# Second-layer products over 512 columns, first-layer row blocks in column groups of their own: an attention and soft-routing kernel on one core

## The chip, the cores and the metric

The kernel runs on one core of a Trainium2 chip. The metric is device time in microseconds (us) from start to end of one execution. The kernel before was timed three times: 200.5, 200.85 and 201.43 us, median 200.85. One execution was also recorded instruction by instruction; all durations below come from that record.

## The reference

Two stages follow each other. The first is an attention with a learned memory: for each of 8 x 8 heads, 576 positions are pooled into 32 memory slots, and the queries attend to those slots. The second is a soft mixture of eight experts over the 4608 rows that come out; the change is in its expert part:

```python
logits = x @ phi                       # x: 4608 x 512, phi: 512 x 32 slots
d = softmax(logits, axis=0)            # over the rows
slot_input = (d.T @ x).reshape(8, 4, 512)
for e in range(8):                     # 4 slots for each expert
    h = np.maximum(slot_input[e] @ w1[e], 0.0)     # 4 x 512 by 512 x 1024
    slot_out[e] = h @ w2[e]                        # 4 x 1024 by 1024 x 512
c = softmax(logits, axis=1)            # over the 32 slots
out = c @ slot_out                     # 4608 x 512
```

w1 and w2 are 16.8 MB each, all fp32. The inputs of the attention are about 33 MB, the output 9.4 MB.

## The kernel before

All data arrives and leaves through one queue, that of SyncE (SP). Its order is fixed when the program is built: attention inputs first, with weight pieces among them, then the rest of w1 and w2, then the stores. Weight pieces lie in a large arena in SBUF; a piece of w2 takes the place of a piece of w1 that TensorE (PE) has finished with, so a load of w2 waits for PE.

First layer (`expert_in`, L1376 to L1394). Each w1 matrix comes as two tiles of 1 MB. A tile holds two blocks of 128 input rows (c = 0, 1), and the 1024 hidden units are dealt into four sets (j). For a tile PE does 8 products of 256 columns. Each has 32 stationary columns (the expert's four slots, the rest zero), and `tile_position` puts the four sets into the four groups of 32 columns of the array. The two row blocks add up in PSUM. Four experts share a bank (EG = 4), so the layer runs in two halves of 64 products.

`hidden` (L1396 to L1421) then turns a half: ScalarE (ACT) copies it out of PSUM with relu, PE does two 128 x 128 transposes, VectorE (DVE) copies the result to hT.

Second layer (`mult`, `expert_out`, `tail_mult`). Each w2 matrix comes in two halves h of 4 row blocks. A product of one half and one half d of the 512 output columns is 4 matmuls of 256 columns in the four column groups, into `pacc[d]` (d = 0 in `kvbank`, d = 1 in `scbank`). Eleven halves are loaded whole. For the last five (NT = 5, the tails) `tail_out` loads the left 256 columns first, ten pieces of 256 KB, and then the right, ten more, so that the left half of the output can leave while the right is still on its way.

`slot_sums(d)` (L1345) copies `pacc[d]` to SBUF (`accs`), sums its four row groups by a product with `rep` (L1357), and splits the result into two fp32r parts in `sr` (L1364, L1369). `direct` (L1587) gives the first output rows straight from `accs`, `half_group` (L1603) the rest of two row groups column half by column half; DVE and ACT evict (L1579, L1580), SP stores (L1616).

The order on each engine is not that of the code: a planner (`Plan.order`) simulates costs given with each `add` and issues in the order that results. PE, ACT and DVE each do their list in order.

Of the kernel before, what the change touches and what calls it, by code (L numbers as in the profile page):

```python
# [253 lines left out]
def act(n, psum=True):  # L254
    return (0.16 if psum else 0.19) + n / 1200.0
# [15 lines left out]
def kernel(  # L271
# [1070 lines left out]
    sr = keep("sr", [P, 2, DM], dtype=F32R, parts=2)  # L1342
    so = [b_l.tile(), Tile(ap=kvbank[:, 1])]

    def slot_sums(d, middle=lambda: None):  # L1345
        x = slice(d * HD, d * HD + HD)
        add(
            *((ACT, act(HD)) if d else (DVE, dve(HD))),
            lambda: (nc.scalar.copy if d else nc.vector.tensor_copy)(
                accs.ap[:, x], pacc[d].ap[:, 0, :HD]  # L1350
            ),
            r=[pacc[d]], w=[accs.part(d)],
        )
# [13 lines left out]
        add(  # L1367
            DVE, dve(HD),
            lambda: nc.vector.tensor_tensor(  # L1369
                sr.ap[:, 1, x], so[d].ap[:, :HD], sr.ap[:, 0, x].bitcast(F32), op=ALU.subtract  # L1370
            ),
            r=[so[d], sr.part(d)], w=[sr.part(d)],
        )
        return z

    def expert_in(e, hb):  # L1376
        w1v = w1[e].rearrange("(i p z) f -> i p (z f)", i=2, z=2)
        w1b = [load_w(w1v[i], wqs if e == EG else ws) for i in range(2)]
        for i in range(2):

            def f(i=i):
                wv = w1b[i].ap.rearrange("p (c f) -> p c f", c=2)
                for c in range(2):
                    for j in range(4):
                        nc.tensor.matmul(  # L1385
                            hb.ap[NS * j: NS * j + NS, :256],
                            SIM.ap[:, 2 * i + c, NS * e: NS * e + NS],
                            wv[:, c].rearrange("p (x j t) -> p x j t", j=4, t=2)[:, :, j, :],
                            start=(e % EG == 0 and i == 0 and c == 0),
                            stop=(e % EG == EG - 1 and i == 1 and c == 1),  # L1390
                            tile_position=(0, NS * j),
                        )

            add(PE, (0.9, 32), f, r=[SIM, w1b[i]], w=[hb])  # L1394

    def hidden(g, hb):  # L1396
        hs, tp = hss.tile(), b_m.tile()

        add(
            ACT, act(256),  # L1400
            lambda: nc.scalar.activation(
                hs.ap.rearrange("p (t x) -> p t x", t=2),
                hb.ap[:, :256].rearrange("p (x t) -> p t x", t=2), AF.Relu,
            ),
            r=[hb], w=[hs],
        )
# [5 lines left out]
        add(PE, 2 * TP, f, r=[hs, ident_b], w=[tp])  # L1412
        x = slice(EG * g, EG * g + EG)
        add(
            DVE, dve(8 * EG * SE),
            lambda: nc.vector.tensor_copy(
                hT().rearrange("p x (e n) -> p x e n", e=E)[:, :, x, :SE],
                tp.ap[:, :256].rearrange("p (x e s) -> p x e s", x=8, e=E)[:, :, x],
            ),
            r=[tp], w=[hTb.part(g)],  # L1420
        )  # L1421

    tails = []

    def mult(dst, e, h, t, d):
        n = 2 if e < ONES else 4
        wide = t.ap.rearrange("p (j t d) -> p j t d", j=n, t=2)
        for k in range(2):
            for j in range(2):
                x, y = 2 * k + j, 2 * h + j  # L1430
                nc.tensor.matmul(
                    dst[NS * x: NS * x + NS, :HD],
                    hT()[:, 4 * k + y, NS * e: NS * e + NS],
                    wide[:, y % n, k, d * HD: d * HD + HD],
                    start=(e == 0 and h == 0),
                    stop=(e == E - 1 and h == 1),
                    tile_position=(0, NS * x),
                )

    def expert_out(e):  # L1440
        w2v = w2[e].rearrange("(p x) d -> p (x d)", x=8)
        if e < ONES:
            for h in range(2):
                t = load_w(w2v[:, h * W_SZ: h * W_SZ + W_SZ])
                for d in range(2):
                    add(
                        PE, (0.45, 16),
                        lambda d=d, h=h, t=t: mult(pacc[d].ap[:, 0], e, h, t, d),
                        r=[hTb.part(e // EG), t], w=[pacc[d]],
                    )  # L1450
            return
        t = w2s.tile().split(8)
        whole = [h for h in range(2) if 2 * e + h < 2 * E - NT]
        if len(whole) == 2:
            load(lambda: t.ap, w2v, 1 << 21, t)
        elif whole:
            load(
                lambda: t.ap[:, :W_SZ], w2v[:, :W_SZ], 1 << 20,
                [x for i in range(4) for x in t.part(i)],
            )  # L1460
        for h in range(2):
            if h not in whole:
                tails.append((e, h, t))
                continue
            for d in range(2):
                add(
                    PE, (0.45, 16),
                    lambda d=d, h=h: mult(pacc[d].ap[:, 0], e, h, t, d),
                    r=[hTb.part(e // EG), *(t.part(4 * h + i) for i in range(4))], w=[pacc[d]],
                )  # L1470

    def tail_out():
        for d in range(2):
# [10 lines left out]
    def tail_mult(d, n, after=()):  # L1484
# [1 line left out]
        return add(  # L1486
            PE, (0.45, 16), lambda: mult(pacc[d].ap[:, 0], e, h, t, d),
            r=[hTb.part(e // EG), *(t.part(4 * h + 2 * d + i) for i in range(2))],
            w=[pacc[d]], after=after,
        )  # L1490


# [69 lines left out]
    for e in range(E):  # L1562
        expert_out(e)
        if e == 0:
            slots(0)
    tail_out()
    for n in range(NT):
        tail_mult(0, n)
    for bp in range(1, NBP):
# [133 lines left out]
```

## Time and profile before

| | us |
|---|---|
| span of the profiled execution | 198.7 |
| its device time | 200.49 |
| median of the three runs | 200.85 |
| lowest, highest | 200.5, 201.43 |
| PE busy | 168.9 (85% of the span) |
| DVE busy | 141.5 (71%) |
| POOL (GpSimd) busy | 95.5 (48%) |
| ACT busy | 74.4 (37%) |

76.47 MB are moved. The profiled time is 0.36 us under the median, and 1.8 us of it lie outside the span. The DMA share of a stretch is the busy time of the 16 DMA engines in it, divided by 16 times its length; packets are counted where they start, so that a short stretch can show more than 1. For each fp32 matmul of the program the trace has two MATMUL records.

### The profile page before, as it was taken

To read this page: it belongs to the slowest core of one execution; us is meant where nothing else is said; L and a number is where in the kernel's file an instruction comes from. 1 tells how busy PE (TensorE), PEld (TensorE's weight loads), DVE (VectorE), ACT (ScalarE), POOL (GpSimd) and SP (SyncE) were. 2 spreads that over 40 slices of the span, in tenths; PEclk is the share of its full clock that TensorE was granted. 3 is DMA by queue.
4 is the path that set the end of the run, shared out by engine and by line. 5 is a ranking of instruction groups with operands and counts; after the bars stand their busy time and mean duration, and the time that the engine had idled before them with its cause. 6 is when DMAs were issued, how large, how long until landed. Compare 5 with 4: busy or idle time off the path is not lost.

```text
span 198.7 us, 6096 instructions
## 1 busy us (share of the span) xinstructions
PE 168.9 (85%) x2607; PEld 107.7 (54%) x2607; DVE 141.5 (71%) x267; ACT 74.4 (37%) x191; POOL 95.5 (48%) x92
## 2 busy tenths in 40 slices
PE   7999747978799899888999888799999998999900
PEld 6677534645457477554666457465555543567500
DVE  7821630699898899999899998368999900558810
ACT  2022314536351665525644243120138510356600
POOL 7199303589993894979964276200005970000000
PEclk9999997999969999999999999999999999999985
DMA  6999999999999999999999999999999999999996
GB/s 198 366 392 393 384 383 390 380 391 378 404 381 386 390 381 407 381 387 402 420 422 411 417 422 421 417 422 434 422 422 422 371 315 322 360 339 343 404 418 297
DMA packets 31642, 76.47 MB, mean 385 GB/s; under 512 B 2048, under 2 KB 15872, under 8 KB 28288
## 3 DMA queue, kind: packets, MB, share of 16 engines
q1 hardware_dynamic: 31616, 76.09, 100.8%
q8 instruction: 20, 0.33, 0.7%
q14 instruction: 6, 0.05, 0.1%
HBM read 66.65 MB, written 9.44 MB: 383 GB/s over the span
## 4 chain that ended last, share of the span: by engine, by line
PE 37%; DMA 20%; DVE 14%; POOL 12%; issue 4%; SPq 4%; ACT 3%; DVEq 0%; POOLq 0%
DMA arena<-in_moe_w_dram 12%; DMA arena<-in_v_dram 9%; PE bank L1603 6%; PE scbank L813 6%; PE kvbank L704 5%; PE bank L882 4%; SPq L502 4%; POOL arena L848 3%; PE bank L1385 3%; POOL arena L871 3%; POOL arena L669 3%; POOL arena L648 3%; PE bank L1010 2%; DVE arena L606 2%; DVE arena L827 2%
## 5 line engine op out<-in xcount | busy, mean ns | idle before, releaser
L648 POOL TENSOR_TENSOR arena<-arena 128x1152 f32<-128x1152 f32 x8 | 21.0, 2632 | 17.5 <-ACT arena L641 14.9
L591 DVE STREAM_TRANSPOSE arena<-top 128x1152 f32<-128x1152 f32 x16 | 21.6, 1354 | 8.2 <-DMA top<-in_q_dram 8.2
L704 PE MATMUL kvbank<-arena 64*32 64x128 f32 x1152 | 20.9, 277 | 6.2 <-issue 2.4
L813 PE MATMUL scbank<-arena 64*64 64x288 f32 x256 | 23.6, 445 | 2.3 <-DVE arena L827 2.3
L520 PE MATMUL kvbank<-ones 128*128 128x256 f32 x82 | 23.3, 421 | 2.4 <-ACT arena L728 1.3
L669 POOL TENSOR_TENSOR arena<-arena 128x128 f32<-128x128 f32 (+2 forms) x32 | 23.3, 730 | 3.2 <-ACT arena L657 1.3
L1541 POOL TENSOR_TENSOR cT<-cS,cT 32x640 fp32r<-32x640 f32 (+1 forms) x8 | 11.3, 1414 | 26.2 <-ACT cT L1536 25.7
L871 POOL TENSOR_TENSOR arena<-arena,ssm 128x576 f32<-128x576 f32 x16 | 18.3, 1152 | 9.5 <-DVE ssm L867 7.9
L704 PEld LDWEIGHTS kvbank<-arena 64*32 64x32 f32 x1152 | 16.5, 107 | 10.8 <-issue 5.4
L848 POOL TENSOR_TENSOR arena<-arena,smx 128x576 f32<-128x576 f32 x16 | 18.4, 1152 | 7.6 <-DVE smx L843 7.6
L606 DVE TENSOR_REDUCE arena<-arena 128x128 f32<-128x1152 f32 x8 | 17.2, 2160 | 4.2 <-DMA arena<-in_phi_dram 4.1
L882 PE MATMUL bank<-arena 128*128 128x288 f32 x64 | 18.7, 425 | 1.0 <-DVE arena L874 0.8
L520 PEld LDWEIGHTS kvbank<-ones 128*128 128x128 f32 x82 | 15.7, 206 | 5.9 <-ACT arena L728 1.7
L1580 DVE COPY arena<-bank 128x256 f32<-128x256 f32 (+1 forms) x30 | 14.4, 510 | 4.9 <-PE bank L1603 3.7
L827 DVE STREAM_TRANSPOSE arena<-scbank 128x576 f32<-128x576 f32 x16 | 12.2, 764 | 5.6 <-PE scbank L813 5.5
L813 PEld LDWEIGHTS scbank<-arena 64*64 64x64 f32 x256 | 10.0, 141 | 10.1 <-DVE arena L827 3.7
L1603 PE MATMUL bank<-sr,cT 64*128 64x256 f32 (+1 forms) x100 | 15.1, 358 | 0.5 <-ACT arena L1579 0.2
L853 ACT ACTIVATE arena<-arena 128x576 f32<-128x576 f32 x16 | 10.9, 684 | 10.9 <-POOL arena L848 10.7
L882 PEld LDWEIGHTS bank<-arena 128*128 128x128 f32 x64 | 11.2, 189 | 6.2 <-DVE arena L874 2.2
L1603 PEld LDWEIGHTS bank<-sr,cT 64*128 64x128 f32 x100 | 9.9, 184 | 6.5 <-DVE arena L1580 4.1
L1579 ACT COPY arena<-bank 128x256 f32<-128x256 f32 (+1 forms) x24 | 10.4, 444 | 8.3 <-PE bank L1603 7.3
L1385 PE MATMUL bank<-arena,SIM 128*32 128x256 f32 x224 | 13.3, 392 | 0.2 <-DVE SIM L1264 0.2
(135 smaller groups left out, 263.6 us busy)
## 6 DMA issues: line engine op xcount, KB each, us to landing
arena<-in_moe_w_dram SPq DMA_DIRECT2D x19, 1024.0 KB, 14.0
top<-in_q_dram SPq DMA_DIRECT2D x8, 1152.0 KB, 12.6
arena<-in_k_dram SPq DMA_DIRECT2D x8, 1152.0 KB, 10.3
arena<-in_v_dram SPq DMA_DIRECT2D x8, 1152.0 KB, 12.7
arena<-in_moe_w_dram SPq DMA_DIRECT2D x3, 2048.0 KB, 14.3
arena<-in_moe_w_dram SPq DMA_DIRECT2D x20, 256.0 KB, 5.7
arena<-in_phi_dram SPq DMA_DIRECT2D x8, 576.0 KB, 7.2
out_dram<-arena SPq DMA_DIRECT2D x10, 384.0 KB, 4.3
```

The lines of the kernel that those rows point to most:

```text
L520: lambda: nc.tensor.matmul(warm.ap, ones, ones.unsqueeze(1).to_broadcast([P, 2, P]), start=True, stop=True,),
L591: lambda: nc.vector.transpose(qT.ap.rearrange("p (i u y) -> p u i y", i=2, y=Y), qt.ap[:, h * QT_SZ: h * QT_SZ + QT_SZ].rearrange("p (u i ...
L606: lambda: nc.vector.tensor_reduce(mx.ap[:, c0:c1], ph().rearrange("p c j m -> p c m j"), axis=AX.X, op=ALU.max),
L648: lambda: nc.gpsimd.tensor_tensor(ph(), ph(), mb.ap[:, c0:c1].unsqueeze(2).to_broadcast([P, c1 - c0, J, M]), op=ALU.subtract,),
L669: plus = lambda o, x, y: nc.gpsimd.tensor_tensor(o, x, y, op=ALU.add)
L704: nc.tensor.matmul(acc.ap[M * c: M * c + M, a, : 2 * D], ph()[h0: h0 + HALF, c, j, :], kv()[h0: h0 + HALF, :, c, j * D: j * D + D], start= ...
L813: nc.tensor.matmul(scb.ap[HALF * g: HALF * g + HALF, a, :JY], pair[g].kd.ap[h0: h0 + HALF, i, c].rearrange("p r m -> p (r m)"), pair[g].qT ...
L848: lambda: nc.gpsimd.tensor_tensor(exv(), exv(), bc(mx), op=ALU.subtract),
L871: lambda: nc.gpsimd.tensor_tensor(exv(), exv(), bc(sm), op=ALU.mult),
L882: nc.tensor.matmul(lp.ap[:, :JY], vpb.ap[:, h, :], aT.ap[:, a * JY: (a + 1) * JY], start=(h == 0), stop=(h == H - 1),)
L1385: nc.tensor.matmul(hb.ap[NS * j: NS * j + NS, :256], SIM.ap[:, 2 * i + c, NS * e: NS * e + NS], wv[:, c].rearrange("p (x j t) -> p x j t", ...
L1603: nc.tensor.matmul(po.ap[:, : x.stop - x.start], cT[bp].ap[y: y + HALF, j // 2 * P: j // 2 * P + P], sr.ap[y: y + HALF, t, x], start=(t == 0),
```

## The change

First layer: a tile now takes 4 products of 512 columns. The two row blocks c no longer add up in PSUM: block c and column set j have a column group of their own, 32 * (2c + j).

`hidden`: ACT copies 512 columns without relu; PE multiplies four 128 x 128 blocks of it (as stationary operand) by `rep2`, 64 columns, two identities one over the other, which turns the block and adds the two row blocks; DVE applies relu while it copies to hT. `rep2` is made by one more DVE reduction. There is one buffer for the copied hidden values where there were two.

Second layer: the eleven whole halves take 4 matmuls of 512 columns each, into the second bank of `scbank`, an accumulator of their own (`wacc` part 1). The tails stay as they were, into `pacc[0]` and `pacc[1]`. `whole_sums` copies the whole halves' sum to `accs` by two ACT copies; its right half is put into `pacc[1]` by a product with the identity ahead of the right tails; its left half is added by DVE in `slot_sums(0)`, where a copy stood.

```diff
-    hss = over([2 * P], 2)
+    hss = over([4 * P], 1)
     hTs = over([8 * E * (NS + SE)], 1)
+    rep2 = over([HALF], 1).tile()
...
+    add(
+        DVE, 0.25,
+        lambda: nc.vector.tensor_reduce(
+            rep2.ap, ident.rearrange("p (c x) -> p x c", c=2), axis=AX.X, op=ALU.add
+        ),
+        r=[ident_b, SIM], w=[rep2],
+    )
...
-    pacc = [b_kv.tile(), b_s2.tile()]
+    wacc = b_s2.tile().split(2)
+    pacc = [b_kv.tile(), wacc]
+    pw = [list(pacc[0]), wacc.part(0)]
...
+            add(
+                DVE, dve(HD),
+                lambda: nc.vector.tensor_tensor(
+                    accs.ap[:, x], pacc[d].ap[:, 0, :HD], wsum()[:, x], op=ALU.add
+                ),
+                r=[pw[d], accs.part(d)], w=[accs.part(d)],
+            )
...
-                    for j in range(4):
+                    for j in range(2):
+                        x = NS * (2 * c + j)
                         nc.tensor.matmul(
-                            hb.ap[NS * j: NS * j + NS, :256],
+                            hb.ap[x: x + NS, :],
                             SIM.ap[:, 2 * i + c, NS * e: NS * e + NS],
-                            wv[:, c].rearrange("p (x j t) -> p x j t", j=4, t=2)[:, :, j, :],
-                            start=(e % EG == 0 and i == 0 and c == 0),
-                            stop=(e % EG == EG - 1 and i == 1 and c == 1),
-                            tile_position=(0, NS * j),
+                            wv[:, c].rearrange("p (x j y) -> p x j y", j=2, y=4)[:, :, j, :],
+                            start=(e % EG == 0 and i == 0),
+                            stop=(e % EG == EG - 1 and i == 1),
+                            tile_position=(0, x),
                         )
...
-            ACT, act(256),
-            lambda: nc.scalar.activation(
-                hs.ap.rearrange("p (t x) -> p t x", t=2),
-                hb.ap[:, :256].rearrange("p (x t) -> p t x", t=2), AF.Relu,
+            ACT, act(512),
+            lambda: nc.scalar.copy(
+                hs.ap.rearrange("p (y x) -> p y x", y=4),
+                hb.ap.rearrange("p (x y) -> p y x", y=4),
             ),
...
-            for t in range(2):
-                nc.tensor.transpose(tp.ap[:, t * P: t * P + P], hs.ap[:, t * P: t * P + P], ident)
+            to = tp.ap[:, :256].rearrange("p (t j i n) -> p t i j n", t=2, j=2, i=2)
+            for y in range(4):
+                nc.tensor.matmul(
+                    to[:, y % 2, y // 2], hs.ap[:, y * P: y * P + P], rep2.ap,
+                    start=True, stop=True,
+                )
...
-                for d in range(2):
-                    add(
-                        PE, (0.45, 16),
-                        lambda d=d, h=h, t=t: mult(pacc[d].ap[:, 0], e, h, t, d),
-                        r=[hTb.part(e // EG), t], w=[pacc[d]],
-                    )
+                add(
+                    PE, (0.9, 16), lambda h=h, t=t: mult(wacc.ap[:, 1], e, h, t),
+                    r=[hTb.part(e // EG), t], w=[wacc.part(1)],
+                )
...
+    def whole_sums():
+        for d in (1, 0):
+            x = slice(d * HD, d * HD + HD)
+            add(
+                ACT, act(HD), lambda x=x: nc.scalar.copy(wsum()[:, x], wacc.ap[:, 1, x]),
+                r=[wacc.part(1)], w=[accs.part(d)],
+            )
+        x = slice(HD, DM)
+        add(
+            PE, 0.45,
+            lambda: nc.tensor.matmul(
+                pacc[1].ap[:, 0, :HD], ident, wsum()[:, x], start=True, stop=False
+            ),
+            r=[accs.part(1), ident_b], w=[pw[1]],
+        )
```

On PE, from the first layer to the first whole halves, the kernel before has this order (L1385 first layer, L1410 transposes, L1431 second layer; `top` and `arena` hold weights, `bank` takes the hidden sums):

```order
L1385 MATMUL bank_62<-arena,SIM 32x256 x64
L1385 MATMUL bank_64<-top,SIM 32x256 x8
L1410 MATMUL bank_63<-ident,arena 128x128 x2
L1385 MATMUL bank_64<-top,SIM 32x256 x8
L1385 MATMUL bank_64<-arena,SIM 32x256 x48
L1431 MATMUL kvbank<-arena 32x256 x4
L1431 MATMUL scbank<-arena 32x256 x4
L1431 MATMUL kvbank<-arena 32x256 x4
L1431 MATMUL scbank<-arena 32x256 x4
L1410 MATMUL bank_62<-ident,arena 128x128 x2
```

After the last of these rows 18 groups of 4 for whole halves and the 20 matmuls of the left tails follow. The changed kernel has, from the same place to the first output rows (L1404 first layer, L1430 the products with rep2, L1455 second layer, L1522 the identity product, L1375 the sum over row groups):

```order
L1404 MATMUL bank_62<-arena,SIM 32x512 x32
L1404 MATMUL bank_64<-top,SIM 32x512 x8
L1430 MATMUL bank_63<-arena 128x2x32 x4
L1404 MATMUL bank_64<-arena,SIM 32x512 x24
L1455 MATMUL scbank<-arena 32x512 x8
L1430 MATMUL bank_62<-arena 128x2x32 x4
L1455 MATMUL scbank<-arena 32x512 x36
L1455 MATMUL kvbank<-arena 32x256 x8
L1522 MATMUL scbank<-cS,ident 128x256
L1455 MATMUL kvbank<-arena 32x256 x12
L1375 MATMUL bank_65<-cS,rep 128x256
```

The first turn has moved behind ten first-layer tiles instead of nine, the whole halves are one run, and the identity product stands between the second and the third left tail. From L1375 on, PE's order is as before.

On ACT, around the second turn and the sums, before (L1401 relu copy, L1536 casts for the routing weights, L1364 the sum's first part):

```order
L1401 ACTIVATE arena<-bank_64 128x256
L1536 CAST cT<-cS 32x640
L1536 CAST cT<-cS 32x512
L1536 CAST cT<-cS 32x640
L1536 CAST cT<-cS 32x512
L1536 CAST cT<-cS 32x640
L1536 CAST cT<-cS 32x512
L1364 CAST sr<-bank_65 128x256
```

And in the changed kernel (L1420, L1572, L1382 are the same three, L1516 the two new copies):

```order
L1420 COPY arena<-bank_64 128x512
L1572 CAST cT<-cS 32x640
L1572 CAST cT<-cS 32x512
L1572 CAST cT<-cS 32x640
L1572 CAST cT<-cS 32x512
L1572 CAST cT<-cS 32x640
L1572 CAST cT<-cS 32x512
L1516 COPY cS<-scbank 128x256 x2
L1382 CAST sr<-bank_65 128x256
```

The two copies stand ahead of the sum's cast. SP issues the same transfers in the same order in both kernels, and POOL's order is unchanged.

## Rows read from the trace of the kernel before

**Rows 1.** The page: the DMA queue's share, and issues of weights (KB each, us to landing).

```profile
q1 hardware_dynamic: 31616, 76.09, 100.8%
...
arena<-in_moe_w_dram SPq DMA_DIRECT2D x19, 1024.0 KB, 14.0
...
arena<-in_moe_w_dram SPq DMA_DIRECT2D x20, 256.0 KB, 5.7
```

**Rows 2.** Windows: length, busy us by engine PE to POOL, clock, DMA share, GB/s.

```profile
136.00:152.00 16.00, 15.79 (x268) 8.79 (x270) 14.79 (x41) 5.08 (x13) 2.71 (x2) 1.00 1.02 429
152.00:160.00 8.00, 8.00 (x146) 4.62 (x142) 6.74 (x22) 5.08 (x10) 5.89 (x6) 1.00 1.00 373
160.00:161.00 1.00, 1.00 (x24) 0.64 (x20) 0.00 (x0) 0.00 (x0) 1.00 (x1) 1.00 0.73 248
161.00:168.00 7.00, 6.07 (x61) 1.78 (x51) 0.42 (x1) 0.00 (x0) 1.71 (x2) 1.00 1.00 326
...
176.00:177.00 1.00, 0.95 (x4) 0.87 (x5) 0.42 (x1) 0.58 (x2) 0.00 (x0) 1.00 0.83 283
177.00:186.00 9.00, 8.73 (x58) 6.21 (x57) 7.32 (x16) 5.49 (x13) 0.00 (x0) 1.00 1.03 347
186.00:197.00 11.00, 3.13 (x15) 1.41 (x13) 3.44 (x6) 2.35 (x4) 0.00 (x0) 0.79 1.04 436
```

**Rows 3.** One tensor's instructions: weight issues on SP, ns min/median/max.

```profile
L502 SPq DMA_DIRECT2D arena<-in_moe_w_dram x42: 327/378/7882, 44.2 to 168.2; - x42
```

**Rows 4.** One line's instructions, L1616: the 19 stores, issue to landing.

```profile
DMA to landing us min/median/max: 2.8/4.3/8.0
```

**Rows 5.** The chain that ended last, from 136 us: start, us, what.

```profile
136.50 6.70 PE bank L1385 x112
143.20 18.03 DMA arena<-in_moe_w_dram
161.25 5.52 DMA arena<-in_moe_w_dram
...
166.81 0.67 PE kvbank L1431 x6
...
167.50 0.43 DVE cS L1349
...
168.68 0.86 PE bank L1587 x4
```

**Rows 6.** Timeline of PE and its weight loads: start, us, [idle before, releaser].

```profile
133.00 1.06 PE L1054 MATMUL bank<-rep,arena 128*128 128x32 f32 x8
136.50 7.56 PE L1385 MATMUL bank<-arena,SIM 128*32 128x256 f32 x128 [0.21 <-DVE SIM L1264]
143.86 1.12 PE L1385 MATMUL bank<-top,SIM 128*32 128x256 f32 x16
...
157.42 0.61 PE L1431 MATMUL kvbank<-arena 128*32 128x256 f32 x8
...
161.31 0.61 PE L1431 MATMUL scbank<-arena 128*32 128x256 f32 x8
...
161.74 5.70 PE L1431 MATMUL kvbank<-arena 128*32 128x256 f32 x40
...
165.42 0.15 PEld L1431 LDWEIGHTS kvbank<-arena 128*32 128x32 f32 x6 [0.52 <-DMA arena<-in_moe_w_dram]
166.81 0.15 PEld L1431 LDWEIGHTS kvbank<-arena 128*32 128x32 f32 x6 [0.55 <-DMA arena<-in_moe_w_dram]
```

**Rows 7.** Groups by shape on ACT, from 143 us: busy, mean ns | idle before.

```profile
L1579 ACT COPY arena<-bank 128x512 f32<-128x512 f32 x8 | 4.7, 587 | 2.4 <-PE bank L1603 2.3
...
L1349 ACT COPY cS<-scbank 128x256 f32<-128x256 f32 x1 | 0.4, 372 | 0.2 <-PE scbank L1431 0.2
```

**Rows 8.** Groups by shape on DVE, from 136 us: busy, mean ns | idle before.

```profile
L1349 DVE COPY cS<-kvbank 128x256 f32<-128x256 f32 x1 | 0.4, 424 | 8.4 <-PE kvbank L1431 8.4
L1369 DVE TENSOR_TENSOR sr<-bank,sr 128x256 fp32r<-128x256 f32 x1 | 0.4, 424 | 1.2 <-ACT sr L1364 1.2
```

More of the change, by code (lines that the diff above doesn't have):

```diff
@@ L1342 @@
     sr = keep("sr", [P, 2, DM], dtype=F32R, parts=2)
+    wsum = lambda: accs.ap
     so = [b_l.tile(), Tile(ap=kvbank[:, 1])]
@@ L1346, in slot_sums @@
         x = slice(d * HD, d * HD + HD)
-        add(
[L1348 to L1352, printed above, removed]
-        )
+        if d:
+            add(
+                ACT, act(HD), lambda: nc.scalar.copy(accs.ap[:, x], pacc[d].ap[:, 0, :HD]),
+                r=[pw[d]], w=[accs.part(d)],
+            )
+        else:
+            add(
[5 more added lines that the diff above has]
+            )
         y = middle()
@@ L1408, in f @@
         def f():
-            for t in range(2):
-                nc.tensor.transpose(tp.ap[:, t * P: t * P + P], hs.ap[:, t * P: t * P + P], ident)
-        add(PE, 2 * TP, f, r=[hs, ident_b], w=[tp])
+            to = tp.ap[:, :256].rearrange("p (t j i n) -> p t i j n", t=2, j=2, i=2)
[4 more added lines that the diff above has]
+                )
+        add(PE, (0.8, 16), f, r=[hs, rep2], w=[tp])
         x = slice(EG * g, EG * g + EG)
@@ L1415, in hidden @@
             DVE, dve(8 * EG * SE),
-            lambda: nc.vector.tensor_copy(
+            lambda: nc.vector.tensor_scalar(
                 hT().rearrange("p x (e n) -> p x e n", e=E)[:, :, x, :SE],
                 tp.ap[:, :256].rearrange("p (x e s) -> p x e s", x=8, e=E)[:, :, x],
+                0.0, None, op0=ALU.max,
             ),
@@ L1423, with mult @@
     tails = []
-    def mult(dst, e, h, t, d):
+    def mult(dst, e, h, t, d=None):
         n = 2 if e < ONES else 4
@@ L1431, in mult @@
                 nc.tensor.matmul(
-                    dst[NS * x: NS * x + NS, :HD],
+                    dst[NS * x: NS * x + NS, : DM if d is None else HD],
                     hT()[:, 4 * k + y, NS * e: NS * e + NS],
-                    wide[:, y % n, k, d * HD: d * HD + HD],
-                    start=(e == 0 and h == 0),
-                    stop=(e == E - 1 and h == 1),
+                    wide[:, y % n, k] if d is None else wide[:, y % n, k, d * HD: d * HD + HD],
+                    start=(d is None and e == 0 and h == 0) or (d == 0 and 2 * e + h == 2 * E - NT),
+                    stop=(2 * e + h == 2 * E - NT - 1) or (e == E - 1 and h == 1),
                     tile_position=(0, NS * x),
@@ L1444, in expert_out @@
                 t = load_w(w2v[:, h * W_SZ: h * W_SZ + W_SZ])
-                for d in range(2):
-                    add(
-                        PE, (0.45, 16),
-                        lambda d=d, h=h, t=t: mult(pacc[d].ap[:, 0], e, h, t, d),
-                        r=[hTb.part(e // EG), t], w=[pacc[d]],
-                    )
+                add(
+                    PE, (0.9, 16), lambda h=h, t=t: mult(wacc.ap[:, 1], e, h, t),
+                    r=[hTb.part(e // EG), t], w=[wacc.part(1)],
+                )
             return
@@ L1464, in expert_out @@
                 continue
[L1465 to L1470, printed above, removed]
+            add(
+                PE, (0.9, 16), lambda h=h: mult(wacc.ap[:, 1], e, h, t),
+                r=[hTb.part(e // EG), *(t.part(4 * h + i) for i in range(4))], w=[wacc.part(1)],
+            )
     def tail_out():
@@ L1488, in tail_mult @@
             r=[hTb.part(e // EG), *(t.part(4 * h + 2 * d + i) for i in range(2))],
-            w=[pacc[d]], after=after,
+            w=[pw[d]], after=after,
+        )
+    def whole_sums():
+        for d in (1, 0):
+            x = slice(d * HD, d * HD + HD)
+            add(
+                ACT, act(HD), lambda x=x: nc.scalar.copy(wsum()[:, x], wacc.ap[:, 1, x]),
+                r=[wacc.part(1)], w=[accs.part(d)],
+            )
+        x = slice(HD, DM)
+        add(
+            PE, 0.45,
[3 more added lines that the diff above has]
+            r=[accs.part(1), ident_b], w=[pw[1]],
         )
@@ L1566 @@
     tail_out()
+    whole_sums()
     for n in range(NT):
```

2 lines of the change are left out of this document (1 added, 1 removed).

## The prediction

> **What bounds the kernel now.** I read the DMA queue first. Its packets take 100.8% of the time that 16 engines have in the span [rows 1], so the question for every change is whether it gives the queue fewer bytes, quicker packets or fewer gaps. The windows say where the gaps are: the DMA share is 1.00 or more in nearly every stretch from 136 us to 197, and only two single microseconds fall short, 160 to 161 with 0.73 and 176 to 177 with 0.83 [rows 2]. The rate does change, at a full share: 429 GB/s while 1 MB and 2 MB pieces arrive, 326 and 347 while the 256-column pieces and half-row stores go, 436 at the end with the wide stores [rows 2]. That is the size of the packets, which the change leaves alone.
>
> The transfers are also far ahead of the engines. A weight piece of 1 MB lands 14.0 us after its issue (median), a piece of 256 KB 5.7 us after [rows 1]; one issue stayed 7.88 us in SP's hands where the median is 378 ns [rows 3], which fits a full queue. Stores need between 2.8 and 8.0 us, median 4.3 [rows 4]: a store of the median kind has about 4.3 - 2.8 = 1.5 us of other transfers ahead of it.
>
> Then the chain that ended last. It seems to tell another story: PE's first layer from 136.50 to 143.20, an 18.03 us transfer, one of 5.52 us, the last left tail at 166.81, the sum on DVE at 167.50 [rows 5]. But the 18.03 us are queue: the piece issued at 143.20 landed when the bytes ahead of it were through. An issue that comes a little earlier only waits longer. What PE waits for at the end is data: before the fourth and the fifth left tail it is released by the transfer, at 165.42 and 166.81 [rows 6], and between 161 and 168 it is busy 6.07 of 7 us in overlapped records [rows 2] for 20 matmuls that, at the pace below, need 2.2 us. So PE has room ahead of the point where the end is decided.
>
> **The change, part by part.** The pace of now first. In the first layer 8 tiles go from 136.50 to 143.86, 7.36 us, so 0.92 us a tile [rows 6]. In the second layer a group of four 256-column matmuls (8 records) takes (161.31 - 157.42) / 9 = 0.432 us, and each such row lasts 0.61 us because neighbours overlap [rows 6].
>
> *First layer, 16 tiles.* Eight matmuls of 256 columns become four of 512: the same columns for the array. If the four column groups overlap as now, a tile costs at best 2 x 0.432 = 0.864 us, and 0.92 if the interleaved reading of the weights keeps its price. I take 0.92, the row of the same line. The worst end, no overlap at all, is 4 x 0.864 = 3.46 us; that is a rival below.
>
> *The two turns.* Each is now four fp32 products with a full stationary block and 64 columns, 8 records. The row nearest is L1054, 8 records of 128x128 on 32 columns, 1.06 us [rows 6]; L1587's two products on 256 columns take 0.86 us [rows 5], so four take 1.72. I take 1.06 and keep 1.72; lower costs would change nothing. ACT's copy in front grows to 512 columns, 587 ns by the evictions of that size [rows 7]; the strided order may double it. Two first-layer tiles (1.84 us) cover the first, two whole halves (1.73 us) the second. The single buffer for the hidden values makes the second copy wait for the first turn, which is six tiles earlier, so for nothing. The relu moves to a DVE instruction that was a copy. The reduction that makes `rep2` runs on DVE, which is busy 0.42 us between 161 and 168 [rows 2]: anything it adds is absorbed there at the latest.
>
> *Second layer, 11 whole halves.* Twice 0.432 becomes once 0.864: nothing.
>
> Added up from 136.50: ten tiles 9.20, turn 1.06, six tiles 5.52, two halves 1.73, turn 1.06, nine halves 7.78, together 26.35; PE comes to the left tails at 162.85, where it came at 161.74 [rows 6]. With 0.864 for a tile it is 161.95, with 1.72 for a turn 164.17.
>
> *The new sum.* Two ACT copies of 372 ns [rows 7] follow the last whole half and end at about 163.7. Behind them in ACT's list stands the sum's cast, which has work only after 168. PE does two tails (to 163.71), the identity product, 0.43 us (half of L1587's 0.86 [rows 5]), to 164.14, the third tail to 164.57, and then waits for data again: fourth tail 165.42, fifth 166.81, as before. Behind the identity product three tails are queued and DVE waits for them; it delays them only if PE is not through with the fourth tail by 166.81, that is, if the whole halves end after 166.81 - 5 x 0.432 = 164.65. Forecast 162.85, slack 1.8 us. If that cover were gone, every microsecond would go into the left sum. On DVE a copy of 128x256 from PSUM (424 ns) becomes an addition with one operand in PSUM; L1369 is of that form and takes 424 ns [rows 8]. Nothing. The right sum is copied as before.
>
> *Transfers.* SP's order is the same. Its loads of w2 wait for first-layer tiles; with 0.864 a tile the sixth or seventh would be released 0.4 us sooner, into a queue of 14 to 18 us. Nothing, except that a gap could be filled: at most 0.27 us at 160 and 0.17 us at 176 [rows 2]. A second turn that ends late can't open one, since the loads wait for tiles only.
>
> Sum: 0. The profiled execution took 200.49 us, 0.36 under the median of 200.85. Between these, nearer the median: **200.8 us**.
>
> **A rule weighed.** The 256-column pieces run at 326 GB/s with a share of 1.00, the large ones at 429 with 1.02 [rows 2]; so the engines are occupied, not waiting. The Trainium skill, "DMA: Bandwidth & Descriptors", section "Specifications", puts the least transfer for line rate at 512 B. By that rule packets of 256 fp32 (1 KB) would be at full rate already. The trace doesn't agree for these pieces: 326 against 429 GB/s.
>
> **The rivals.**
>
> *Starved queue, faster.* The slow stretches could be stretches in which SP issues too late because PE frees buffers too late, and the busy share could hide it. Then, against 436 GB/s, 7 x (1 - 326/436) = 1.8 us of 161 to 168 and 9 x (1 - 347/436) = 1.8 us of 177 to 186 could come back, at most 3.6 us: 197.2. For it speaks the chain through L1385; against it the shares of 1.00 and 1.03 and the 5.7 us to landing. The rule above would have it this way. Chance 0.04.
>
> *The chain taken at its word, a little faster.* Seven tiles at 0.864 save 0.4 us before 143.20, and both gaps close, 0.44 us: 200.0. That is within what a measurement of this kernel can tell from no change, 0.5%, about 1.0 us. Chance 0.10.
>
> *Overlap lost, slower.* No row shows 512 columns in four column groups. If a group of four costs over 0.864 us, the whole halves come late. It decides from (164.65 - 136.50 - 2.12) / 27 = 0.964 us a step, over 16 tiles and 11 halves. At a quarter more than full overlap, 1.08 us, they end at 136.50 + 27 x 1.08 + 2.12 = 167.78, six groups of 0.432 later the left sum can start at 170.37 instead of 167.24, 3.1 us late; 1.5 us of queued transfers cover part, and 1.6 us remain: 202.5. For it: the first layer already pays 0.92 where the second pays 0.864. Against it: one product of 256 columns on the whole array takes 0.43 us [rows 5], and four of 256 columns in the column groups take 0.432 us together [rows 6], which is full overlap. Chance 0.08.
> The Trainium skill, "TensorE: Matmul & The Clock Gate", section "Part 3: Packing small matmuls — row/col tiling", gives three column groups at 512 columns a speedup of 2.38, not 3. By that a step would be 0.864 x 3 / 2.38 = 1.09 us (an estimate), and the time about 202.7. The trace disagrees at 256 columns, with 0.43 us for one and 0.432 us for four; no row here shows it at 512.
>
> **How the numbers follow.** No change by the sum above 0.78, the small gain 0.10, lost overlap 0.08, starved queue 0.04. The three runs before spread from 200.5 to 201.43, so the forecast's own range is 200.2 to 201.6; it is drawn out to the small gain on one side and half the slow rival on the other: 199.9 to 201.9. Faster by over 0.5% takes the starved queue and a fifth of the small gain, 0.06. Slower by over 0.5% takes the lost overlap and 0.02 for an unforeseen wait in the left sum, 0.10. Within 0.5%: 0.84.
>
> **What would show it.** In the profile after: 64 first-layer matmuls at about 0.92 us for four, and whole halves at 0.864; the left tails begun at about 162.9 and the fifth still released by its transfer at about 166.8; the addition at about 167.5; a DMA share of about 1 from 136 to 197 with the same rates, 436 GB/s at the end. Wrong is the forecast if steps cost over 0.96 us, if the fifth tail is released by PE or ACT, or if a new gap stands in the DMA share between 150 and 185.

## The result, and the profile after

The changed kernel takes 202.25 us (median of 4 runs, 202.19 to 202.7); the kernel before, on the same chip, 200.88 (4 runs, 200.5 to 201.43). The ratio is 1.0069, 95% interval [1.0047, 1.009]: slower, by 1.4 us. All medians in this document are of all runs, all ratios of the fast runs alone (those over 1.5% above the fastest of their kernel are left out), so that a kernel whose runs spread has a smaller ratio than its median suggests. Forecast were 200.8 us, and 199.9 to 201.9 as the range. The prediction was wrong.

The profiled execution took 202.27 us with a span of 200.5, 1.78 us over the 200.49 of before. The page after, its engines, its queues and the issues of weights:

```profile
PE 169.6 (85%) x2405; PEld 102.9 (51%) x2405; DVE 141.5 (71%) x268; ACT 75.6 (38%) x193; POOL 95.5 (48%) x92
...
q1 hardware_dynamic: 31616, 76.09, 100.1%
q8 instruction: 19, 0.31, 0.6%
...
arena<-in_moe_w_dram SPq DMA_DIRECT2D x19, 1024.0 KB, 14.2
...
arena<-in_moe_w_dram SPq DMA_DIRECT2D x20, 256.0 KB, 5.9
```

The data queue moved the same packets and bytes as in [rows 1], and its pieces need as long to land. The same lines of the page before:

```profile
PE 168.9 (85%) x2607; PEld 107.7 (54%) x2607; DVE 141.5 (71%) x267; ACT 74.4 (37%) x191; POOL 95.5 (48%) x92
...
q8 instruction: 20, 0.33, 0.7%
```

The program has 103 TensorE products fewer, each four records (two products and two weight loads), and 404 of the 412 show in these rows; the second queue, "instruction", has one packet of 16 KB fewer. I had not read that line before the prediction. The windows after, cut as in [rows 2]; columns: length, busy us of PE, PEld, DVE, ACT, POOL, granted clock, DMA share, GB/s.

```profile
136.00:152.00 16.00, 15.79 (x142) 5.24 (x145) 14.80 (x42) 5.14 (x12) 2.45 (x2) 1.00 1.02 430
152.00:160.00 8.00, 7.88 (x76) 2.94 (x72) 7.10 (x23) 5.34 (x11) 5.74 (x5) 1.00 1.00 378
160.00:161.00 1.00, 1.00 (x14) 0.26 (x8) 0.00 (x0) 0.19 (x1) 0.93 (x2) 1.00 0.94 308
161.00:168.00 7.00, 6.37 (x58) 2.00 (x50) 0.12 (x1) 0.65 (x2) 2.16 (x2) 1.00 1.04 339
...
176.00:177.00 1.00, 0.89 (x6) 0.66 (x7) 0.42 (x1) 0.72 (x2) 0.00 (x0) 1.00 1.02 347
177.00:186.00 9.00, 8.73 (x57) 6.21 (x58) 6.90 (x16) 5.71 (x13) 0.00 (x0) 1.00 0.99 329
186.00:197.00 11.00, 3.58 (x18) 1.79 (x16) 3.86 (x6) 2.35 (x4) 0.00 (x0) 0.75 1.03 427
197.00:200.50 3.50, 0.00 (x0) 0.00 (x0) 0.00 (x0) 0.00 (x0) 0.00 (x0) 0.50 0.19 79
```

Up to 197 us these rows give the picture of before: a share of about 1, the same slow and fast stretches. New is the last row: 3.5 us at a share of 0.19, in which no engine computes. Finer windows show two short gaps that the kernel before does not have (after, then before):

```profile
172.00:173.00 1.00, 1.00 (x14) 0.49 (x14) 0.42 (x1) 0.00 (x0) 0.00 (x0) 1.00 0.79 270
179.00:181.00 2.00, 1.98 (x18) 1.57 (x17) 1.78 (x5) 1.14 (x4) 0.00 (x0) 1.00 0.85 279
```

```profile
172.00:173.00 1.00, 1.00 (x16) 0.54 (x8) 0.38 (x2) 0.18 (x1) 0.00 (x0) 1.00 1.10 372
179.00:181.00 2.00, 1.99 (x19) 1.65 (x16) 1.57 (x6) 1.12 (x4) 0.00 (x0) 1.00 1.01 337
```

A new gap between 150 and 185 us was a sign of being wrong in the prediction, and it came. It is not what makes this loss: `first_only` below has the second gap too (0.88 from 179 to 181) and another at 174 (0.81), and is not slower. The chain that ended last, after (start, us, what; compare [rows 5]):

```profile
136.67 6.71 PE bank L1404 x61
143.39 17.90 DMA arena<-in_moe_w_dram
161.30 5.78 DMA arena<-in_moe_w_dram
167.12 0.67 PE kvbank L1455 x6
...
167.88 0.44 DVE cS L1367
```

It is the old chain, step by step, 0.17 us later at its start and 0.38 us later at the sum (167.50 before). And the timeline after, with the idle time before a row and its releaser in brackets (compare [rows 6 to 8]):

```profile
136.67 7.07 PE L1404 MATMUL bank<-arena,SIM 128*32 128x512 f32 x64 [0.21 <-DVE SIM L1264]
...
143.56 1.90 PE L1404 MATMUL bank<-top,SIM 128*32 128x512 f32 x16
...
145.39 1.10 PE L1430 MATMUL bank<-arena 128*128 128x64 f32 x8
...
154.66 7.93 PE L1455 MATMUL scbank<-arena 128*32 128x512 f32 x72
...
162.41 1.05 PE L1455 MATMUL kvbank<-arena 128*32 128x256 f32 x16
...
162.66 0.65 ACT L1516 COPY cS<-scbank 128x256 f32<-128x256 f32 x2 [2.47 <-PE scbank L1455]
...
163.38 0.70 PE L1522 MATMUL scbank<-cS,ident 128*128 128x256 f32 x2
...
165.65 0.15 PEld L1455 LDWEIGHTS kvbank<-arena 128*32 128x32 f32 x6 [0.57 <-DMA arena<-in_moe_w_dram]
...
167.12 0.15 PEld L1455 LDWEIGHTS kvbank<-arena 128*32 128x32 f32 x6 [0.61 <-DMA arena<-in_moe_w_dram]
167.88 0.42 DVE L1367 TENSOR_TENSOR cS<-kvbank,cS 128x256 f32<-128x256 f32 x1 [8.35 <-PE kvbank L1455]
```

Every engine did what was forecast: a first-layer tile (143.56 - 136.67) / 8 = 0.86 us, a whole half (162.41 - 154.66) / 9 = 0.86, a turn 1.10, the left tails from 162.41 (forecast 162.85), the fourth and the fifth released by their transfers, the addition 0.42 us. None of these is the greater part of the loss.

**Where it is.** The stores end the program. All 19, issue to landing, after (compare [rows 4]):

```profile
DMA to landing us min/median/max: 2.1/3.8/9.2
```

The longest is the last, 2304 KB. It was issued at 190.37 us (before: 189.92) and took 9.24 us (before: 7.96). So, between these two executions, 0.45 us are lateness at the issue and 1.28 us are the store itself, together 1.73 of 1.78. The end in windows, after and then before, columns as above:

```profile
195.00:197.00 2.00, 0.00 (x0) 0.00 (x0) 0.00 (x0) 0.00 (x0) 0.00 (x0) 0.50 0.97 415
197.00:198.00 1.00, 0.00 (x0) 0.00 (x0) 0.00 (x0) 0.00 (x0) 0.00 (x0) 0.50 0.61 258
198.00:199.00 1.00, 0.00 (x0) 0.00 (x0) 0.00 (x0) 0.00 (x0) 0.00 (x0) 0.50 0.04 18
```

```profile
195.00:197.00 2.00, 0.00 (x0) 0.00 (x0) 0.00 (x0) 0.00 (x0) 0.00 (x0) 0.50 1.04 442
197.00:198.00 1.00, 0.00 (x0) 0.00 (x0) 0.00 (x0) 0.00 (x0) 0.00 (x0) 0.50 0.01 0
198.00:198.70 0.70, 0.00 (x0) 0.00 (x0) 0.00 (x0) 0.00 (x0) 0.00 (x0) 0.50 0.00 0
```

A packet of this store is 18 KB and takes 0.69 us, and these rows count it where it starts. Before, none of the store's packets starts after 197.0, and the 16 engines are all through by 197.55. After, fifteen are through by about 198.0, and one goes on alone, two packets more, to 199.28; a share of 0.04 is less than one engine in sixteen. The store counts as landed when the last has ended. What did that engine have to do that the others had not? The second queue suggests it. The DMA row of the 0.1 us from 184.75, after (packets, MB, share):

```profile
q1 hardware_dynamic: 33, 0.03, 110.3%
q8 instruction: 1, 0.02, 71.6%
```

That is one packet of 16 KB, TensorE's program code, at 184.8 us (in the runs below, TensorE instructions added or left out change the number of these packets, from 18 to 21); the trace gives it 1.15 us on its engine, while the queue keeps the engines busy. The kernel before has 20 such packets, one per 245 TensorE records on average ((5069 - 421) / 19, counted from the first to the last), the last at 174.6 us. With 412 records fewer the boundaries between the pieces of code fall elsewhere: after, the last packet comes at 184.8, amid the last stores. The Trainium skill, "Runtime: NRT & Kernel Launch", section "Instruction fetch mechanics", has code refilled in 16 KiB blocks of 256 instructions, with the cost of a boundary mostly hidden. The size agrees with this trace, and the count nearly (245 records on average). The cost is hidden in the runs below where the packet comes 13 us or more before the issue of the last store, and not where it comes 5.6 us or less before it.

### The profile page after: what moved, and what is told of

Same layout as the page of the kernel before. It is cut to its first block, busy times and chain, and to the rows that moved or that the text cites. A ratio compares the mean times of both kernels' runs of the same rounds, so it can differ in the third digit from the quotient of the medians.

```text
span 200.5 us, 5698 instructions
## 1 busy us (share of the span) xinstructions
PE 169.6 (85%) x2405; PEld 102.9 (51%) x2405; DVE 141.5 (71%) x268; ACT 75.6 (38%) x193; POOL 95.5 (48%) x92
## 4 chain that ended last, share of the span: by engine, by line
PE 37%; DMA 20%; DVE 14%; POOL 12%; issue 5%; SPq 4%; ACT 3%; DVEq 0%; POOLq 0%; ACTq 0%
DMA arena<-in_moe_w_dram 12%; DMA arena<-in_v_dram 8%; PE bank L1640 6%; PE scbank L813 5%; PE kvbank L704 5%; SPq L502 4%; PE bank L882 4%; POOL arena L848 3%; PE bank L1404 3%; POOL arena L871 3%; POOL arena L669 3%; POOL arena L648 3%; PE bank L1010 2%; DVE arena L606 2%; DVE arena L827 2%
## 5 line engine op out<-in xcount | busy, mean ns | idle before, releaser
L520 PE MATMUL kvbank<-ones 128*128 128x256 f32 x82 | 24.6, 440 | 2.4 <-ACT arena L728 1.3
L813 PE MATMUL scbank<-arena 64*64 64x288 f32 x256 | 23.0, 433 | 2.0 <-DVE arena L827 2.0
L520 PEld LDWEIGHTS kvbank<-ones 128*128 128x128 f32 x82 | 16.5, 216 | 6.4 <-ACT arena L728 1.7
L1616 ACT COPY arena<-bank 128x256 f32<-128x256 f32 (+1 forms) x24 | 10.4, 445 | 8.2 <-PE bank L1640 7.3
L1455 PE MATMUL scbank<-arena 128*32 128x512 f32 (+1 forms) x128 | 13.0, 530 | 0.0
```

What stands on the lines that cost most here:

```text
L520: lambda: nc.tensor.matmul(warm.ap, ones, ones.unsqueeze(1).to_broadcast([P, 2, P]), start=True, stop=True,),
L813: nc.tensor.matmul(scb.ap[HALF * g: HALF * g + HALF, a, :JY], pair[g].kd.ap[h0: h0 + HALF, i, c].rearrange("p r m -> p (r m)"), pair[g].qT ...
```

## Experiments

Theory F: the last packet of program code, if it comes after the queue's last gap (a short time in which the engines have too little to do, so that a late one can catch up), makes one DMA engine late, and the last store waits for it. Rival S: the new sum (or anything else on an engine) makes the stores later. All kernels were timed in five rounds beside the kernel before. The changes to the program code use a product of one column, `tiny`, which is four records; a MATMUL record of it lasts 0.17 us, and 30 products in a row took 2.06 us (`b_end120`):

```
nc.tensor.matmul(warm.ap[:NS, :1], ones[:, :NS], ones[:, :1], start=True, stop=True)
```

**The two halves of the change.** `first_only` has the first layer and its turn, `second_only` the second layer and its sum:

```
first_only:  the change without its lines in pacc, slot_sums, mult, expert_out, whole_sums
second_only: the change without its lines in hss, rep2, expert_in, hidden
```

> Only the first part of the change: first layer in four products of 512 columns and the new turn; the second layer as before. Some 230 PE instructions fewer than before. Fetch theory: the last fetch falls at 172 to 177 us, as before, 200.9 us (200.4 to 201.3). Rival that the first layer's new form costs the time: 202.2 us.

Measured 200.77 us, ratio 0.9985 [0.9964, 1.0006]: as expected, no change. Last fetch 174.3, last store 7.93 us.

> Only the second part of the change: whole halves over 512 columns, their own accumulator, the new sum; first layer and turns as before. Some 170 PE instructions fewer than before. Fetch theory: the last fetch that matters falls at 171 to 173 us, the next block boundary stands at the end of the program: 200.9 us (200.4 to 201.4). Rival that the new sum makes the stores late: 202.2 us.

Measured 202.74 us, ratio 1.009 [1.0067, 1.0112]: slower, against the expectation of 200.4 to 201.4, which took it that no boundary came so near the end. One did. The DMA row of the 0.15 us from 188.95 (packets, MB, share), and then the issue of the last store (KB, us to landing), in the trace of second_only:

```profile
q8 instruction: 1, 0.02, 38.7%
```

```profile
out_dram<-arena SPq DMA_DIRECT2D x1, 2304.0 KB, 9.7
```

The packet at 189.0 us goes with a last store of 9.73 us, while the sum (167.69 us) and the stores (first 169.74, last 190.16) are within 0.04 us of those of first_only. So S has nothing to go by; the expectation failed in where it placed the boundary.

**The sum made later by itself.** In the kernel before, the left sum's copy is made twice:

```
-            lambda: (nc.scalar.copy if d else nc.vector.tensor_copy)(
-                accs.ap[:, x], pacc[d].ap[:, 0, :HD]
-            ),
+            lambda: [
+                (nc.scalar.copy if d else nc.vector.tensor_copy)(...)
+                for _ in range(1 if d else 2)
+            ],
```

> The kernel before with the left sum's copy on DVE made twice (0.42 us more before the sum over row groups), so that every store is issued 0.4 us later, as in the changed kernel; PE's instructions are untouched. Fetch theory: 200.9 to 201.3 us, since the queue covers most of it. Late-stores rival: 202.2 us.

Measured 201.32 us, ratio 1.0022 [1.0011, 1.0034], last fetch 175.9, last store 8.05 us. A sum 0.42 us later costs 0.2%, 0.4 us (0.2 to 0.7 by the interval): most or all of it. The last store hardly gets longer (7.96 before). So a late sum is paid for the most part, which I had not believed, and 0.4 us are still only a third of the loss.

**Code moved from the start.** In the changed kernel 20 of the 41 warm-up products, early ones, left out (80 records); or 45 tiny products added among them (180); in the kernel before, 26 added (104):

```
a_minus80:  + if 4 < fills[0] <= 24: return
a_plus180:  + for _ in range(3 if 4 < fills[0] <= 19 else 0): <tiny>
b_plus104:  + for _ in range(2 if 4 < fills[0] <= 17 else 0): <tiny>
```

> The changed kernel with 20 of its 41 warm-up products left out (80 PE instructions fewer; they fill a scratch area, no result depends on them). Fetch theory: a block of PE program code (16 KB, fetched on the same DMA engines, 1.15 us on one of them) at 184.8 us delays one engine in the last stores; 80 instructions fewer push that block boundary behind the end, the last fetch falls at about 174 us, and the time is that of the kernel before, 200.9 us (200.5 to 201.3). Late-stores rival: the stores are late by 0.4 us because of the new sum and the queue runs dry; nothing of that is touched here, so 202.2 us.

> The changed kernel with 45 tiny products (one column, scratch output) added among the first warm-up products: 180 PE instructions more. Fetch theory: the block boundaries come 180 instructions sooner, the last fetch at about 173 us instead of 184.8: 200.9 us (200.5 to 201.3). Late-stores rival: 202.2 us, nothing near the end is touched.

> The kernel before with 26 tiny products added among the first warm-up products: 104 PE instructions more, so that block boundaries fall where the changed kernel has them, fetches at about 170 and 185 us. Fetch theory: 202.2 us (201.7 to 202.6), with a last store that lands late behind one engine. Late-stores rival: 200.9 us, the stores are where they were.

Measured 205.14 (ratio 1.0219 [1.0192, 1.0247]), 210.63 (1.0342 [1.0294, 1.0389]) and 205.25 (1.0199 [1.0168, 1.023]). All three times miss: the body of the program suffers, with first stores at 172.87, 180.62 and 172.65 us where the kernel before has 169.54. As a test of times they are lost. Their ends still say something: a_minus80 has its last fetch at 177.7 and a last store of 7.92 us with all engines ending together; b_plus104 has it at 190.5 and 9.49 us, one engine alone at the end. a_plus180 has it at 183.8, 17 us before its late last store is issued, and 7.91 us.

**Code moved from the middle.** Warm-ups between 116 and 136 us, each replaced by five tiny products: ten of them in the changed kernel, seven in the kernel before.

```
-    (warm-up product, 128 x 256)
+    if 31 < fills[0] <= 41:      # a_mid160;  b_mid112: 34 < fills[0] <= 41
+        for _ in range(5): <tiny>
```

> The changed kernel with the ten warm-up products between 116 and 136 us each replaced by five tiny ones (one column, scratch output): 160 PE instructions more, at about the same PE time, so that the blocks of program code keep their places until 116 us and come 160 instructions sooner after it. Fetch theory: the last code fetch moves from 184.8 to about 174 us, the last store lands about 8.0 us after its issue instead of 9.2, and the time is 200.9 to 201.4 us. Rival, the new sum and its stores alone: 202.2 us.

> The kernel before with the last seven warm-up products each replaced by five tiny ones: 112 PE instructions more after 127 us. Fetch theory: the 20th fetch moves from 174.6 to about 169 us and a 21st comes at about 184 to 186; the last store takes 9.2 us or more to land instead of 8.0 and the time is 202.0 to 202.5 us. Rival, the new sum and its stores: 200.9 us, since nothing of them is here.

b_mid112 is as expected: 202.17 us, ratio 1.0055 [1.0035, 1.0075]; a 21st fetch at 184.6, a last store of 9.27 us. Its granted clock was 0.50 from 136 to 140 us (1.00 in the kernel before), but its stores are late by 0.3 us only (first 169.83, last 190.21), so the clock does not explain the time. a_mid160 missed in time, 205.81 us, ratio 1.0131 [1.0079, 1.0182], and not in its end (last fetch 178.0, last store 7.90). Its windows, columns as above:

```profile
135.00:140.00 5.00, 4.84 (x71) 4.58 (x70) 2.76 (x10) 0.00 (x0) 0.00 (x0) 0.50 1.03 426
140.00:145.00 5.00, 4.88 (x24) 1.19 (x28) 4.46 (x9) 0.56 (x2) 0.00 (x0) 0.50 0.88 352
```

The granted clock is at its 1.2 GHz level (0.50) in the first layer, where it is 1.00 in the changed kernel; that layer takes longer, and the first store is issued at 173.60.

**Code behind everything.** The cleanest trial: the kernel before, with 30 tiny products behind its last product. Nothing waits for them, and nothing stands behind them; in the trace they run from 189.18 to 191.24 us. (`z` is the last product.)

```
+    def tiny():
+        for _ in range(30): <tiny>
+    add(PE, 0.5, tiny, r=[ones_b], w=[warm], after=[z])
```

> The kernel before, with 30 one-column products (120 TensorE instructions) behind its last product, at about 189.6 us; nothing waits for them, and every other instruction keeps its place. Program-code theory: 120 more instructions bring a 21st fetch of 16 KB between 189 and 194 us, while the last store (2304 KB, issued at 189.9) is on its way; the engine that carries it ends about 1.1 to 1.3 us after the others, the store takes 9.0 to 9.4 us instead of 7.96, and the time is 202.0 to 202.4. Rival (the later second sum, or anything else on an engine, costs the time): nothing on an engine is later here, so 200.9, store 7.9 to 8.0 us.

Measured 203.11 us, ratio 1.0094 [1.0059, 1.0128]: slower as expected, but beyond the 202.0 to 202.4. The last store was issued at 190.04, 0.12 us later than before. The DMA rows of the 0.2 us from 192.5, the last store's, and the windows at the end, in the trace of b_end120:

```profile
q8 instruction: 1, 0.02, 29.1%
```

```profile
out_dram<-arena SPq DMA_DIRECT2D x1, 2304.0 KB, 9.8
```

```profile
195.00:197.00 2.00, 0.00 (x0) 0.00 (x0) 0.00 (x0) 0.00 (x0) 0.00 (x0) 0.50 1.04 442
197.00:198.00 1.00, 0.00 (x0) 0.00 (x0) 0.00 (x0) 0.00 (x0) 0.00 (x0) 0.50 0.05 18
198.00:199.00 1.00, 0.00 (x0) 0.00 (x0) 0.00 (x0) 0.00 (x0) 0.00 (x0) 0.50 0.09 37
```

Fifteen engines are through by about 197.6, and one goes on to 199.4. The store takes 9.81 us, more than the 9.0 to 9.4 that I had expected, and the program 1.9 us more by the ratio (2.1 by the medians), for instructions that no other instruction waits for. That is F, and S can't explain it.

**Code added at the end of the changed kernel.** 12 tiny products where TensorE waits for the fourth and fifth left tail; then 12 more, one ahead of each of the first output products:

```
+    tiny(6 if d == 0 and n >= NT - 2 else 0), mult(pacc[d].ap[:, 0], e, h, t, d)
+    tiny(1 if outs[0] <= 12 else 0)        # a_tail96, in out_mult
```

> The changed kernel, with 12 one-column products (48 TensorE instructions) ahead of the fourth and fifth left tails, where TensorE waits for data. Program-code theory: the last fetch moves from 184.8 to about 182; whether the delayed engine makes up by the end is open at that distance, so the last store takes between 7.9 and 9.2 us and the time is 200.9 to 202.2. Rival: 202.2 or a little more, with the store at 9.2 us.

> As the one before, and one more such product ahead of each of the first 12 output products (96 instructions in all). Program-code theory: the last fetch moves to about 179, where the runs with their last fetch at 174 to 178 had no store held up: last store 7.9 to 8.0 us, no engine alone at the end, time 200.9 to 201.5 (the 12 small products in the output loop may make some stores later by up to 0.5 us). Rival: 202.2 or more, since only work is added.

a_tail48: 201.86 us (12 runs, 201.39 to 204.27), ratio 1.0044 [1.0015, 1.0073], five of the 12 at 201.4 or 201.5, which the changed kernel reached in none of its 4. The profile happened to be taken of the slowest run, with its first layer 2.3 and its stores 2.7 us late; there the last fetch came 9.2 us before the last store's issue (5.6 in the changed kernel), and the store took 8.55 us, between the two values, as F left open. a_tail96 missed in time, 206.23 us, ratio 1.0166 [1.0115, 1.0217]. Its windows, columns as above:

```profile
176.00:180.00 4.00, 4.00 (x37) 2.76 (x36) 1.70 (x4) 1.12 (x3) 0.00 (x0) 0.78 0.59 197
180.00:184.00 4.00, 4.00 (x18) 2.35 (x10) 1.27 (x3) 1.12 (x3) 0.00 (x0) 0.50 0.59 201
```

The output loop with the small products in it went at a share of 0.59, with the clock falling to its lower level (0.50), and the last store was issued at 196.63. I had put that cost at 0.5 us. Its end is as F has it: last fetch 180.3, store 7.73 us, all engines together.

**The same 96 records, earlier.** As a_mid160, with six of the warm-ups replaced and the last four kept:

```
+    if 31 < fills[0] <= 37:
+        for _ in range(5): <tiny>
```

> The changed kernel, with six of its warm-up products between 116 and 130 us (fills 32 to 37 of 41) each replaced by five one-column products: 96 more TensorE instructions, in place and time of work that nothing waits for, and the four last warm-ups kept so that the granted clock should stay at 1.00 in the first layer. Program-code theory: the last fetch moves from 184.8 to about 179, the last store (issued at about 190.3) takes 7.9 to 8.0 us instead of 9.24, all engines end together, and the time is 200.9 to 201.5. Rival (the change's own lateness of some engine): 202.2, with the store still at 9.2. If the clock falls as it did with ten warm-ups replaced, the stores are issued later and the time tells nothing, and only the store's duration does.

Measured 202.51 us (12 runs, 200.78 to 205.92), ratio 1.0053 [1.0022, 1.0084]. The median missed the 200.9 to 201.5 and shows no gain over the changed kernel's 202.25: the runs spread widely, with mean granted clocks of 0.912 to 0.955 (0.961 in the changed kernel's profile). The trace of one of them, of 201.53 us: the first layer, then the end in windows, then the last store.

```profile
139.34 7.07 PE L1411 MATMUL bank<-arena,SIM 128*32 128x512 f32 x64 [0.21 <-DVE SIM L1271]
```

```profile
195.00:197.00 2.00, 0.00 (x0) 0.00 (x0) 0.00 (x0) 0.00 (x0) 0.00 (x0) 0.50 0.97 415
197.00:198.00 1.00, 0.00 (x0) 0.00 (x0) 0.00 (x0) 0.00 (x0) 0.00 (x0) 0.50 1.12 479
198.00:199.00 1.00, 0.00 (x0) 0.00 (x0) 0.00 (x0) 0.00 (x0) 0.00 (x0) 0.50 0.01 0
```

```profile
out_dram<-arena SPq DMA_DIRECT2D x1, 2304.0 KB, 8.0
```

The last fetch came at 177.8. Although its first layer began 2.7 us later than the changed kernel's and its last store was issued 0.54 us later, it ended 0.7 us sooner (store landed at 198.89 against 199.62), because the store took 7.98 us and all engines ended together.

**All ends side by side** (profiled runs, us; the interval is from the last fetch to the issue of the last store; "queue short" is the start of the last whole microsecond before that issue with a DMA share of at most 0.92, and its share):

| kernel | last fetch | queue short | last store issued | interval | store took |
|---|---|---|---|---|---|
| a_plus180 | 183.8 | 191 (0.87) | 201.06 | 17.3 | 7.91 |
| a_tail96 | 180.3 | 186 (0.80) | 196.63 | 16.3 | 7.73 |
| a_mid160 | 178.0 | 179 (0.61) | 194.05 | 16.1 | 7.90 |
| first_only | 174.3 | 180 (0.86) | 190.12 | 15.8 | 7.93 |
| a_minus80 | 177.7 | 183 (0.84) | 193.33 | 15.6 | 7.92 |
| before | 174.6 | 176 (0.83) | 189.92 | 15.4 | 7.96 |
| b_late_sum | 175.9 | 181 (0.91) | 190.69 | 14.8 | 8.05 |
| a_mid96 | 177.8 | 180 (0.85) | 190.91 | 13.1 | 7.98 |
| a_tail48 | 183.9 | 183 (0.88) | 193.10 | 9.2 | 8.55 |
| b_mid112 | 184.6 | 180 (0.82) | 190.21 | 5.6 | 9.27 |
| after | 184.8 | 180 (0.81) | 190.37 | 5.6 | 9.24 |
| b_plus104 | 190.5 | 182 (0.92) | 193.03 | 2.5 | 9.49 |
| second_only | 189.0 | 180 (0.85) | 190.16 | 1.1 | 9.73 |
| b_end120 | 192.6 | 176 (0.85) | 190.04 | -2.6 | 9.81 |

From 13 us up the store takes 7.7 to 8.05 us, in a kernel before or after; at 5.6 us or less 9.2 to 9.8. Whether a row has the whole change, half of it or none makes no difference. The column "queue short" parts the kernels in the same way: in the eight with a short store the queue fell short once more after the last fetch, in the five with a long one it did not, and in a_tail48 the fetch came as the last gap ended. These windows were read after the runs, and no run tells the distance from the gap. No version here beats the kernel before; first_only equals it.

## Why the prediction was wrong

**The products** were right in kind, and the tile better than taken: 0.86 us, not 0.92, so 512 columns in four column groups overlap in full, and "overlap lost" is refuted (it needed over 0.964). Right too: the turn (1.10 for 1.06), the sums' copies on ACT (ended at 163.31, forecast 163.7), the identity product in TensorE's wait, the tails released by data, the addition at the price of the copy. "Starved queue" is not seen: with TensorE as early as forecast, 161 to 168 still runs at 339 GB/s. The stretches at 160 and 176 did fill up (0.73 to 0.94, 0.83 to 1.02), others opened at 172 and 179, and nothing was gained at the end.

**The step that failed** is "Transfers": "SP's order is the same." and then "Nothing, except that a gap could be filled". It counted as transfers only what SP issues. TensorE's own code comes over the same engines, and a change that takes 103 products away moves it, though no instruction is moved in the queue. The share of about 1 up to 197 us was in its rows, so a further transfer there could hardly be free; I did not ask which transfers there are besides SP's. The page's line on "instruction", 20 packets, said so. The 1.28 us of the longer store are this step's; b_end120 gives the step its price by itself, and a_mid96 ends without it.

**"Sum: 0."** also left out 0.45 us of lateness at the stores. 0.17 of it stood there when the first layer began, before the changed products, and the addition was 0.38 us late mostly because the fifth piece came 0.31 us late (167.12 against 166.81). first_only and second_only issue their last stores at 190.12 and 190.16, also later than before's 189.92, and first_only is not slower. Much of it may be the choice of execution: the profiled one of before was 0.39 us under its median (200.49 against 200.88), that of after 0.02 over its own, and the medians differ by 1.37 us, 0.1 more than the 1.28 of the store. No run tells what share of the 0.45 us belongs to the change; that stays open.

**An estimate that fell.** In the slow rival I let 1.5 us of queued transfers cover a late sum. b_late_sum shows little or no cover: 0.42 us later at the sum, 0.4 us (0.2 to 0.7) later at the end.

## What to carry to other kernels

Where the end of a program is a queue of large stores, read the page's second queue too: a packet of program code that comes after the queue's last gap delays one engine, and the last store waits for the slowest. A change in the number of TensorE's instructions (the only engine tried), even of idle ones, moves these packets, so a difference of one or two us between two versions can come from where a boundary falls, and adding instructions that nothing waits for is a way to tell. And if instructions are added or left out to move a boundary, look at the granted clock and the first stores before the time.

## What the runs showed of the hardware

- A 16 KB packet of TensorE's code took 0.88 to 1.43 us (in all traces after 164 us) on a DMA engine that also carries data. Late in the program it cost a store of 2304 KB 1.3 us (fetched 5.6 us ahead of its issue) to 1.9 us (fetched while it ran); fetched 13 us or more ahead, with a gap in the queue after it, the store took 7.7 to 8.05 us as in the kernel before. Why the 1.9 us are more than the packet itself (0.93 us in b_end120) is open. The records don't name the engine, so that the one left alone is the one that fetched is inferred, from b_end120 above all.
- Four products of 512 columns in four column groups take 0.86 us together, the time of two such groups at 256 columns (0.432 each, [rows 6]).
- With ten of the last warm-ups replaced by one-column products the granted clock was 0.50, its 1.2 GHz level, from 135 to 145 us (a_mid160), with the last seven replaced it was 0.50 from 136 to 140 (b_mid112); with six replaced and the last four kept it was 1.00 from 136 to 162 us (a_mid96).
- A share of the DMA engines of about 1 does not tell that no engine is behind: from 195 to 197 us b_end120 has 1.04 as the kernel before has, and its late engine shows only after 197, when the others have nothing left to do.
